# Attention issued from a dated list, with mirrored blocks loaded whole, in a float32 attention and two feed-forward stages on one core

## The chip, the cores and the metric

The kernel runs on one core of a Trainium2 chip. The metric is the device time of one execution in microseconds (us). Five instruction streams run beside each other: TensorE (PE, with its weight loads shown as PEld), VectorE (DVE), ScalarE (ACT), the sync engine (SP, which here only issues DMAs), and GpSimd (POOL, unused but for six instructions). Each stream runs its instructions strictly in the order in which the program lists them; an instruction that has to wait holds up all behind it on its engine.

## The reference

There are two batches of 3008 rows; z has 64 columns, v and u have 256. Scores are taken of z against itself, so the score matrix is symmetric.

```python
scores = (z @ z.T) / S                 # S = 3008
attn   = np.maximum(scores, 0.0) ** 2
x      = u * (attn @ v)                # (2*3008, 256)
h = np.maximum(x @ w_in, 0.0);  x = (h * h) @ w_out            # 2048 hidden columns
h = x @ w2_in;                  y = (h - np.tanh(h)) @ w2_out  # 2048 hidden columns
```

The weights of both feed-forward stages come in float64; the rest is float32.

## The kernel before

Every product of two float32 values is made of three matmuls on operands of TensorE's rounded type fp32r: a value a is split into h (the rounded value) and l = a - h, and h*h, h*l and l*h are summed in PSUM. Splitting is work for ACT (a copy with rounding, or a DVE cast) and DVE (the subtraction).

**Attention.** The 3008 query columns of a batch are cut into six chunks (t = 0 to 5) of 512 columns, the last of 448; with two batches there are twelve chunks. A chunk has twelve *steps*, one for each pair of blocks of 128 keys. A step ends in `values` (24 matmuls into four PSUM banks, 18 for the last pair). What `values` multiplies is made in one of two ways:

- A **scored** step: `scores` (6 matmuls, L508), ACT Relu from PSUM (L520), ACT Square (L544), the rounded copy h on ACT (L548) or DVE (L556), the rest l on DVE (L557). Where the chunk lies left of the diagonal, `put` stores the squared block in DRAM (`ad`).
- A **mirrored** step: since the matrix is symmetric, a chunk t takes its first 2t pairs from what earlier chunks stored. `get` (L463) loads the pair from `ad` with four DMAs, DVE turns it in blocks of 32x32 (`turn`, L472), ACT makes h (L477), DVE makes l (L492).

So chunk t has 12 - 2t scored and 2t mirrored steps, 84 and 60 in all. At a chunk's end ACT and DVE copy the four banks to SBUF (L596, L597), DVE adds the two halves (L600) and multiplies by u (L603), and the product goes to DRAM (`xd`).

**Beside attention** run the splits of v and z, and of the feed-forward weights: one *weight unit* is 128 hidden columns of one stage, loaded as float64 words, decoded and split by six DVE and three ACT instructions (L232 to L245). There are 32 units. The first 6 stay in SBUF, the next `KEEP0 + KEEP1` = 14 are made during attention and kept in DRAM (`wd`), and the last 12 are made while the feed-forward stage runs.

**Order.** The main loop goes through the steps; `scores` runs `APART` = 2 steps ahead of `values`, `get` `XAHEAD` = 3 steps ahead of its use. The side work stands in lanes (z, x, v, weights), from which `fill` takes instructions between those of a step, at a pace worked out from due times.

**Feed-forward.** 192 steps of the first stage (`m1`) and 192 of the second (`m2`), 12 matmuls each (`front` L629, `back` L697); `m1` runs 21 steps ahead, then the two alternate.

Of the kernel before, what the change touches and what calls it, by code (L numbers as in the profile page):

```python
# [17 lines left out]
P = 128  # L18
NMAX = 512
LOOK = 3  # L20
APART = 2
# [4 lines left out]
NW, NZ, NRAW = 32, 7, 3  # L26
# [3 lines left out]
STAY, KEEP0, KEEP1 = 6, 6, 8  # L30
XAHEAD = 3
# [10 lines left out]
def kernel(  # L42
# [58 lines left out]
    for t in range(NC):  # L101
        old, own = list(range(2 * t)), list(range(2 * t, NV))
        own = own[2:] + own[:2] if t else own
        spots = {(2 * k + 1) * NV // (2 * len(old)) for k in range(len(old))}
        if 2 in spots:
            spots = (spots - {2}) | {min(set(range(3, NV)) - spots)}
        plist.append([(old if x in spots else own).pop(0) for x in range(NV)])
# [14 lines left out]
    for i in range(len(m2)):  # L122
# [17 lines left out]
        (b, t, k): dp.tile([qch[k][1], NMAX], F32, name="ad")  # L140
# [6 lines left out]
    def load_v(b, j):  # L147

        if b == 0 and 3 <= j < 6:
            raw = rawp.tile([P, 2, D], F32, tag="raw", name="vraw")  # L150
        else:
            raw = ap_.tile([P, 2, D], F32, tag="a", name="vraw")
        if j < NV - 1:
            order = "(p k) d -> p k d" if j < 2 * (NC - 1) else "(k p) d -> p k d"
            SP.dma_start(
                out=raw, in_=v[b, 2 * j * P : 2 * (j + 1) * P, :].rearrange(order, p=P)
            )
# [25 lines left out]
    def split_z(b, t, raw):  # L183
        z = zp.tile([P, 2, NMAX], F32R, tag="z", name="z")
        zt[b, t] = z
# [8 lines left out]
    def load_w(m, f, keep):  # L194
        win, wout = ((w1_in, w1_out), (w2_in, w2_out))[m]
        cols = slice(f * P, (f + 1) * P)
        if win.dtype == F32:
            raw = rawp.tile([P, 512], F32, tag="raw", name="wraw")
# [6 lines left out]
        raw = rawp.tile([P, 1024], U32, tag="raw", name="wraw")  # L205
# [10 lines left out]
    def split_w(m, f, keep, raw):  # L216
        if keep is None:
# [28 lines left out]
        if keep is not None:  # L246
# [6 lines left out]
    def new_xs(m, c):  # L253
        xs[m, c] = tuple(zp.tile([P, KD, NMAX], F32R, tag="z", name=x) for x in ("xh", "xl"))
        return xs[m, c]

    def load_x(c):
# [3 lines left out]
        return x  # L261

    def split_x(c, x):
        n = chunks[c][2]
        xh, xl = new_xs(0, c)
        yield "A", lambda: A.activation(xh[:, :, :n], x[:, :, :n], AF.Copy)
# [55 lines left out]
    v_units, z_units, x_units, k_units = [], [], [], []  # L322
    by_hand = {("z", 0), ("z", 1), ("z", 2), ("v", 0), ("v", 1)}
    for b in range(B):
        base, end = at["att", b * NC, 0], at["att", (b + 1) * NC - 1, 0]
        for j in range(NV):
            start = 0 if b == 0 else at["att", b * NC - 1, 0] + j + APART
            if b or ("v", j) not in by_hand:
                v_units.append((base + j + 1, start, load_v, split_v, (b, j), 2))
        for t in range(NC):  # L330
            i = b * NC + t
            start = 0 if b == 0 else base - 6 + 2 * t
            if b or ("z", t) not in by_hand:
                z_units.append((base + 2 * t, start, load_z, split_z, (b, t), 2))

# [4 lines left out]
    def weights(ids, first, last):  # L340
        for k in ids:
            k_units.append((last, first, load_w, split_w, (*order[k], keeps.get(k)), 9))
    nv = at["att", NC, 0]
    weights(range(STAY + KEEP0), 10, nv - NV)
    split = STAY + KEEP0 + KEEP1
    weights(range(STAY + KEEP0, split), nv + 6, at["m1", 0, 0] - 2)

    end = at["att", NCH - 1, 0]
    for i, k in enumerate(range(STAY, len(order))):
        m, f = order[k]  # L350
        start = end + max(i + APART + 1, 7) if i < NV else at["m1", 0, 0] + 2
        if k < split:
            fetches.append((start, m, f, keeps[k]))
        else:
            k_units.append((at[("m1", "m2")[m], 0, f], start, load_w, split_w, (m, f, None), 9))
    for c in range(NCH):
        need = at["m1", c, 0]
        free = need - 8 if c == 0 else at["m1", c - 1, 0] + 4
        x_units.append((need, free, load_x, split_x, (c,), 3))
    lane_z, lane_v = Lane(z_units, 2, 1), Lane(v_units, 3, 2)  # L360
    lanes = [lane_z, Lane(x_units, 1, 1), lane_v, Lane(k_units, NRAW, 2)]
# [21 lines left out]
    got = {}  # L383
    single = {}
# [42 lines left out]
    def load_u(i):  # L427

        _, c, x = steps[i]
        b, q, n = chunks[c]  # L430
        if x == 4:
            xt[c] = xp.tile([P, KD, NMAX], F32, tag="x", name="x")
            t0 = b * S + q
            SP.dma_start(
                out=xt[c][:, :, :n],
                in_=uT[:, t0 : t0 + n].rearrange("(k p) t -> p k t", p=P),
            )

    def put(i, a):
# [3 lines left out]
        k = p // 2  # L443
        if k == t:
            return
        r0, tail = p % 2 * 2 * P, p == NV - 1
        rows = ad[b, t, k][r0 : min(r0 + 2 * P, qch[k][1]), :]
        if tail:
            SP.dma_start(out=rows[:P], in_=a[:, 0, :])
            SP.dma_start(out=rows[P:], in_=a[:TAIL, 1, :])  # L450
        else:
            order = "(p k) q -> p k q" if k < NC - 1 else "(k p) q -> p k q"
            SP.dma_start(out=rows.rearrange(order, p=P), in_=a)

    def get(i):

        _, c, _ = steps[i]
        b, t, p = c // NC, c % NC, pair_of(i)
        nb = chunks[c][2] // 32
# [4 lines left out]
        got[i] = m  # L464

    def turn(i):

        _, c, _ = steps[i]
        n = chunks[c][2]
        m = got.pop(i)  # L470
        a = wp.tile([P, 2, NMAX], F32, tag="w", name="at")
        V.transpose(  # L472
            a[:, :, :n].rearrange("p g (k j) -> p k g j", j=32),
            m[:, : n // 32, :].rearrange("p k (i g) -> p k g i", g=2),
        )
        h = wp.tile([P, 2, NMAX], F32R, tag="w", name="ht")
        A.activation(h[:, :, :n], a[:, :, :n], AF.Copy)  # L477
        got[i] = (a, h)

    def low(i):  # L480

        _, c, _ = steps[i]
        n = chunks[c][2]
        a, h = got.pop(i)
        l = wp.tile([P, 2, NMAX], F32R, tag="w", name="l2")
        pair[i] = (h, l)
        credit[0] = min(4, credit[0] + pace(i))
        if late:
            late.popleft()()
        else:  # L490
            credit[0] -= fill(i, min(2, math.ceil(credit[0])), "VS")
        V.tensor_sub(l[:, :, :n], a[:, :, :n], h[:, :, :n])  # L492
        credit[0] -= fill(i, min(2, math.ceil(credit[0])), "A")

    def scores(i):
# [19 lines left out]
        a = wp.tile([P, 2, NMAX], F32, tag="w", name="a2")  # L515
        if i == 0:
            A.activation(a[:, 0, :], both[0], AF.Relu, scale=scale)
            V.tensor_scalar(a[:, 1, :], both[1], scale, 0.0, op0=ALU.mult, op1=ALU.max)
        else:
            A.activation(a[:, :, :n], s[:, :, :n], AF.Relu, scale=scale)  # L520
        return a

    def squares(i, a):

        _, c, x = steps[i]
        n = chunks[c][2]
        full = a
        a = a[:, :, :n]
        h = hp.tile([P, 2, NMAX], F32R, tag="h", name="h2")
        l = wp.tile([P, 2, NMAX], F32R, tag="w", name="l2")  # L530
        pair[i] = (h, l)
        if i == 0:

            A.activation(h[:, 0, :], a[:, 0, :], AF.Square)
            first("z", 1)
            V.tensor_mul(a[:, 1, :], a[:, 1, :], a[:, 1, :])
            first("v", 0)
            A.activation(a[:, 0, :], a[:, 0, :], AF.Square)
            V.tensor_copy(h[:, 1, :], a[:, 1, :])
            first("v", 0)  # L540
            for g in (1, 0):
                V.tensor_sub(l[:, g, :], a[:, g, :], h[:, g, :])
            return
        A.activation(a, a, AF.Square)  # L544
        put(i, full)
        turned = c % NC > 1 or c % NC == 1 and x % 2
        if turned:
            A.activation(h[:, :, :n], a, AF.Copy)  # L548
        credit[0] = min(4, credit[0] + pace(i))

        if late:
            late.popleft()()
        else:
            credit[0] -= fill(i, min(2, math.ceil(credit[0])), "VS")
        if not turned:
            V.tensor_copy(h[:, :, :n], a)  # L556
        V.tensor_sub(l[:, :, :n], a, h[:, :, :n])  # L557
# [275 lines left out]
```

## Time and profile before

| | |
|---|---|
| median of 3 runs | 1577.77 us (1576.92 to 1579.72) |
| profiled execution: its own time | 1580.93 us |
| its span, first to last instruction | 1579.1 us |
| attention: up to the first matmul of `m1` (L629) | 521.7 us |
| feed-forward: from there to the end | 1057.4 us |
| PE busy | 1510.7 us (96%), 8512 matmuls |
| DVE, ACT busy | 1227.6 us (78%), 1057.1 us (67%) |

The profiled execution is one run of its own; its time is 3.2 us above the median. Busy time counts any moment at which an instruction of the engine runs. [...]

### The profile page before, as it was taken

Reading aid. Unit: us, or ns where it says so; the run is one execution under the profiler, and the core shown is the slowest. Engines: PE = TensorE matmul, PEld = TensorE weight load, DVE = VectorE, ACT = ScalarE, POOL = GpSimd, SP = SyncE. Lnnn points to the kernel's source line nnn. Section 1 sums busy time; section 2 is a strip of 40 time slices with the busy share of each in tenths; the row PEclk is TensorE's granted clock in tenths of the full one; section 3 lists DMA queues with packets and bytes.
Section 4 is the critical chain, followed back from the end, with each engine's and each line's share of the span. In section 5 each row is a group of like instructions: output and inputs, shape, how many; then the busy total and the mean of one; then the engine's idle time right before and its main releaser. Section 6 shows DMA issues by size and latency. Waiting matters only on the chain.

```text
span 1579.1 us, 22289 instructions
## 1 busy us (share of the span) xinstructions
PE 1510.7 (96%) x8512; PEld 1250.7 (79%) x8512; DVE 1227.6 (78%) x1897; ACT 1057.1 (67%) x1664; POOL 0.3 (0%) x6
## 2 busy tenths in 40 slices
PE   9989888999888999689999999999999999999999
PEld 7767667777677888578888888888888888888888
DVE  7777778787666689667877788877778787778788
ACT  8777656777654577456766666666666676666688
POOL 0000000000000000000000000000000000000000
PEclk9999999999999999899999999999999999999999
DMA  7767877777797521000000000000000000000000
GB/s 245 222 185 179 195 185 186 233 223 210 185 201 190 185 67 42 12 27 1 26 1 1 27 0 28 0 28 0 26 1 27 1 26 1 1 14 1 14 1 26
DMA packets 166698, 127.27 MB, mean 81 GB/s; under 512 B 126144, under 2 KB 137792, under 8 KB 166592
## 3 DMA queue, kind: packets, MB, share of 16 engines
q1 hardware_dynamic: 166288, 125.48, 28.5%
q8 instruction: 66, 1.08, 0.3%
q10 hardware_dynamic: 304, 0.38, 0.1%
q14 instruction: 40, 0.33, 0.1%
HBM read 76.02 MB, written 49.81 MB: 80 GB/s over the span
## 4 chain that ended last, share of the span: by engine, by line
PE 76%; DVE 6%; ACT 6%; DMA 5%; SPq 4%; issue 2%; DVEq 0%; ACTq 0%
PE s L629 33%; PE o L697 32%; PE o L584 9%; DMA m<-ad 4%; SPq L463 3%; DVE at L472 2%; ACT a L544 2%; PE s L508 2%; ACT h L548 1%; ACT ht L477 1%; DVE l L557 1%; DVE l L492 1%; DMA zraw<-in_z_dram 1%; DVE e L597 0%; DVE mant L242 0%
## 5 line engine op out<-in xcount | busy, mean ns | idle before, releaser
L697 PE MATMUL o<-h,ww 128*128 128x512 f32 (+1 forms) x2304 | 579.2, 387 | 0.0
L697 PEld LDWEIGHTS o<-h,ww 128*128 128x128 f32 x2304 | 435.0, 189 | 83.1 <-DVE h L677 0.5
L629 PE MATMUL s<-xh,ww 128*128 128x512 f32 (+1 forms) x1536 | 408.2, 388 | 17.4 <-ACT ww L244 14.8
L629 PEld LDWEIGHTS s<-xh,ww 128*128 128x128 f32 x1536 | 289.6, 189 | 73.6 <-ACT ww L244 16.0
L584 PE MATMUL o<-l,vw 64*128 64x512 f32 (+1 forms) x1128 | 236.5, 402 | 20.9 <-DVE l L557 12.3
L644 DVE TENSOR_TENSOR h<-a,h 128x512 fp32r<-128x512 f32 (+1 forms) x192 | 130.6, 680 | 141.4 <-ACT h L642 141.1
L584 PE MATMUL o<-h,vw 64*128 64x512 f32 (+1 forms) x1296 | 211.4, 402 | 24.8 <-ACT h L548 19.3
L629 PE MATMUL s<-xl,ww 128*128 128x512 f32 (+1 forms) x768 | 235.0, 387 | 0.0
L637 ACT ACTIVATE a<-s 128x512 f32<-128x512 f32 (+1 forms) x192 | 113.0, 589 | 180.7 <-PE s L629 179.6
L656 ACT ACTIVATE f<-s 128x512 f32<-128x512 f32 (+1 forms) x192 | 114.5, 596 | 129.0 <-PE s L629 129.0
L584 PEld LDWEIGHTS o<-h,vw 64*128 64x128 f32 x1296 | 129.2, 191 | 59.5 <-ACT h L548 27.2
L629 PEld LDWEIGHTS s<-xl,ww 128*128 128x128 f32 x768 | 145.0, 189 | 27.3
L557 DVE TENSOR_TENSOR l<-a,h 128x1024 fp32r<-128x1024 f32 (+1 forms) x83 | 101.2, 1219 | 82.5 <-ACT h L548 81.2
L584 PEld LDWEIGHTS o<-l,vw 64*128 64x128 f32 x1128 | 117.7, 191 | 56.0 <-DVE l L557 25.8
L659 DVE TENSOR_TENSOR a<-s,a 128x512 f32<-128x512 f32 (+1 forms) x192 | 130.4, 679 | 37.8 <-ACT a L657 25.6
L584 PE MATMUL o<-ht,vw 64*128 64x512 f32 (+1 forms) x960 | 150.4, 385 | 0.0
L477 ACT ACTIVATE ht<-at 128x1024 fp32r<-128x1024 f32 (+1 forms) x60 | 61.6, 1027 | 122.8 <-DVE at L472 119.6
L675 DVE COPY_PREDICATED a<-small,f 128x512 f32<-128x512 uint8 (+1 forms) x171 | 126.9, 742 | 5.5
L638 ACT ACTIVATE a<-a 128x512 f32<-128x512 f32 (+1 forms) x192 | 119.7, 624 | 6.1
L678 DVE TENSOR_TENSOR h<-a,h 128x512 fp32r<-128x512 f32 (+1 forms) x172 | 117.9, 686 | 5.9
L672 DVE TENSOR_TENSOR f<-s,f 128x512 f32<-128x512 f32 (+1 forms) x171 | 117.2, 685 | 5.8
L658 ACT ACTIVATE f<-f 128x512 f32<-128x512 f32 (+1 forms) x192 | 121.5, 633 | 0.0
(65 smaller groups left out, 1414.9 us busy)
## 6 DMA issues: line engine op xcount, KB each, us to landing
ad<-a SPq DMA_DIRECT2D x50, 512.0 KB, 3.1
m<-ad SPq DMA_DIRECT2D x160, 128.0 KB, 4.1
m<-ad SPq DMA_DIRECT2D x80, 112.0 KB, 4.2
wraw<-in_moe_w_in_dram SPq DMA_DIRECT2D x32, 256.0 KB, 4.2
wraw<-in_moe_w_out_dram SPq DMA_DIRECT2D x32, 256.0 KB, 4.5
wd<-wk SPq DMA_DIRECT2D x14, 512.0 KB, 4.4
ww<-wd SPq DMA_DIRECT2D x14, 512.0 KB, 6.8
vraw<-in_v_dram SPq DMA_DIRECT2D x22, 256.0 KB, 3.9
```

Source lines behind the costliest of these rows:

```text
L557: V.tensor_sub(l[:, :, :n], a, h[:, :, :n])
L584: T.matmul(o[r * KD + d][:, :n], lhsT=w[halves[r], hl, g * D + d * P : g * D + (d + 1) * P], rhs=mv[halves[r], g, :n], start=x == 0 and (r ...
L629: T.matmul(s_, lhsT=w[:, hl, kd * P : (kd + 1) * P], rhs=mv[:, kd, :n], start=j == 0, stop=j == len(seq) - 1,)
L638: A.activation(a_, a_, AF.Square)
L644: main.append(lambda: V.tensor_sub(l[:, :n], a_, h[:, :n]))
L656: A.activation(f_, s_, AF.Tanh, scale=TB)
L658: A.activation(f_, f_, AF.Square, scale=TC)
L659: main = [lambda: V.tensor_sub(a_, s_, a_)]
L672: main.append(lambda: V.tensor_mul(g_, s_, f_))
L675: late.append(lambda: V.copy_predicated(a_, mask, g_))
L678: late.append(lambda: V.tensor_sub(l[:, :n], a_, h[:, :n]))
L697: T.matmul(o[d][:, :n], lhsT=w[:, side, (KD + d) * P : (KD + d + 1) * P], rhs=mv, start=k == 0 and j == 0, stop=k == NF - 1 and j == len(t ...
```

## The change

In the attention part, the order in which instructions stand on PE, ACT, DVE and SP no longer comes from the main loop and its lanes. Each piece of work is a `Job` with a key (the date at which it is wanted), the jobs that it must follow with a lag, the buffers that it takes and gives back, and a cost on its engine. `drive` walks a model of the four queues in time: whichever engine can start a job first takes the ready one with the smallest key, and only then the instruction is written into the program. The order of PE is a fixed list in which `scores` stands `APART` = 3 steps ahead. A rounded copy of a scored step may go to ACT or DVE, whichever takes it first. The feed-forward part keeps the loop and the lanes.

Further:

- A square of 512 x 512 scores is stored as one DRAM block of 1 MB. `put` writes a pair as four pieces of 1 KB in each partition; `get` loads a whole block, two pairs, with one DMA of 8 KB in each partition. A `turn` reads its pair out of that block with a step of 4 words and writes with a step of 16 words (before: reads with a step of 2, writes runs of 32). In the chunk of 448 columns a `turn` is two instructions of 512. Keys of z are read by the weight loads of `scores` with a step of 4 words (before 2), and rows of v are permuted to match.
- At a chunk's end `values` is cut in two halves by output bank. ACT copies one bank (L603) and DVE adds the other straight from PSUM (L605); the add L600 is gone. For chunks 4 to 11 the product with u moves to the feed-forward stage (`split_x`), which loads u there.
- `KEEP1` goes from 8 to 12: 18 units are kept in DRAM in place of 14, and 8 in place of 12 are made in the feed-forward stage. Pools: 4 z buffers of 8 KB a partition (before 7 of 4 KB), 2 raw buffers (before 3); half of the late weight loads land in the pool `w`.

```diff
-APART = 2
+APART = 3
-NW, NZ, NRAW = 32, 7, 3
+NW, NZ, NRAW = 32, 4, 2
-STAY, KEEP0, KEEP1 = 6, 6, 8
-XAHEAD = 3
+STAY, KEEP0, KEEP1 = 6, 6, 12
+LANES = 8
+EARLY = 4
...
-        (b, t, k): dp.tile([qch[k][1], NMAX], F32, name="ad")
+        (b, t, k): dp.tile([4, P, 4, P], F32, name="ad")
...
+        if c >= EARLY:
+            yield "V", lambda: V.tensor_mul(x[:, :, :n], x[:, :, :n], u[:, :, :n])
         yield "A", lambda: A.activation(xh[:, :, :n], x[:, :, :n], AF.Copy)
...
-        z = z[:, p % 2 * 2 * P : (p % 2 + 1) * 2 * P]
         if p < 2 * (NC - 1):
-            return z.rearrange("r (p k) -> r k p", k=2)[:, g]
-        return z[:, g * P : (g + 1) * P]
+            return z.rearrange("r (p t k) -> r t k p", t=2, k=2)[:, p % 2, g]
+        k = p % 2 * 2 + g
+        return z[:, k * P : (k + 1) * P]
...
-        m = zp.tile([P, 2 * NMAX // 64, 64], F32, tag="z", name="m")
-        rows = ad[b, p // 2, t].rearrange("(k j) (t a x) -> t a j k x", j=32, a=4, t=2)[p % 2]
-        for g in range(4):
-            SP.dma_start(out=m[g * 32 : (g + 1) * 32, :nb, :], in_=rows[g])
...
+        rows = ad[b, t, p // 2].rearrange("a p (t k) x -> t p a (k x)", t=2)[p % 2]
+        SP.dma_start(out=rows, in_=sq[i].rearrange("p a g x -> p a (g x)"))
...
+        m = zp.tile([P, 4 * 4, P], F32, tag="z", name="m")
+        rows = ad[block].rearrange("a (j m) k x -> (a j) (m k x)", m=4)
+        SP.dma_start(out=m.rearrange("p k x -> p (k x)"), in_=rows)
...
+        if c % NC < NC - 1:
+            V.transpose(
+                a.rearrange("p g (j k) -> p k g j", k=16),
+                m.rearrange("p k (i t g) -> t p k g i", t=2, g=2)[p % 2],
+            )
+        else:
+            for g in range(2):
+                V.transpose(
...
+        if e == "A":
+            A.activation(s, o[d][:, :n], AF.Copy)
+        else:
+            V.tensor_add(s, o[KD + d][:, :n], s)
...
+        found = [(max(free[e], ready(j)), j) for j in jobs]
+        start = min(t for t, _ in found)
...
+        soon = [(j.key, t, k) for k, (t, j) in enumerate(found) if t <= start + 0.5]
+        key, t, k = min(soon)
...
+        while any(queue.values()):
+            options = [(*x, e) for e in "PAVS" if (x := best(e)) is not None]
+            t, job, e = min(options, key=lambda x: x[0])
...
+            job.run(e, pools)
+            free[e] = t + cost
+            job.done = t + cost + 0.06
...
+                if block not in blocks:
+                    lim = 1 if t == 1 else 2
...
+                        after.append((blocks[older[-lim]][1], 0.0))
+                    after.append(((max(i - 8, 0)), 0.0))
+                    load = Job(
+                        lambda e, pools: get(block), need - 14.0, after, ["z"], S=3.0
+                    )
```

Where instructions stand now, in three places.

SP, in chunk 4 of the first batch (t = 4), before. L463 is `get`, L434 the load of u, L207 and L211 the loads of a weight unit, L247 its store:

```order
L604 DMA xd<-x 128x1024
L463 DMA m<-ad 32x16x64 x4
L434 DMA x<-in_u_dram 128x2x512
L247 DMA wd<-wk 128x1024
L207 DMA wraw<-in_moe_w_in_dram 128x2x256
L211 DMA wraw<-in_moe_w_out_dram 128x512
L463 DMA m<-ad 32x16x64 x8
L247 DMA wd<-wk 128x1024
L463 DMA m<-ad 32x16x64 x4
L463 DMA m<-ad 32x14x64 x8
```

The same place of the changed kernel; L446 is `get`, L215 and L219 load and L974 stores a weight unit:

```order
L616 DMA xd<-x 128x1024
L215 DMA wraw<-in_moe_w_in_dram 128x2x256
L219 DMA wraw<-in_moe_w_out_dram 128x512
L974 DMA wd<-wk 128x1024
L446 DMA m<-ad 128x2048 x2
L974 DMA wd<-wk 128x1024
```

Before, each pair of blocks takes four loads; now one load brings two pairs, and weight stores stand between the loads.

ACT in the same chunk, before, from one scored step's Relu (L520) to its rounded copy (L548); L477 is the rounded copy of a mirrored step, L234 and L235 belong to a weight unit:

```order
L477 ACTIVATE ht<-at 128x1024
L234 ACTIVATE mant<-mant 128x512
L235 ACTIVATE exp<-exp,ebias 128x512
L520 ACTIVATE a_2497<-s 128x1024
L477 ACTIVATE ht<-at 128x1024
L544 ACTIVATE a_2497<-a_2497 128x1024
L548 ACTIVATE h_2527<-a_2497 128x1024
```

ACT around the corresponding scored step of the changed kernel; L507 is the Relu, L518 the Square, L487 the rounded copy of either kind:

```order
L507 ACTIVATE a_2500<-s 128x2x4x128
L518 ACTIVATE a_2500<-a_2500 128x1024
L487 ACTIVATE h_2509<-at 128x1024
L487 ACTIVATE h_2535<-a_2500 128x1024
L487 ACTIVATE h_2541<-at 128x1024
L242 ACTIVATE mant<-mant 128x512
L243 ACTIVATE exp<-exp,ebias 128x512
```

Before, a mirrored step's copy stands between the Relu and the Square of a scored step; now the Square follows the Relu, and a mirrored step's copy stands behind the Square.

DVE in the first chunk of the feed-forward stage, before, with the eleventh weight unit made there (L232 to L245) between the instructions of an `m1` step (L644) and `m2` steps (L659 to L678):

```order
L644 TENSOR_TENSOR h<-a,h 128x512
L677 CAST h<-a 128x512
L678 TENSOR_TENSOR h<-a,h 128x512
L232 TENSOR_SCALAR mant<-wraw 128x512
L233 TENSOR_SCALAR exp<-wraw 128x512
L236 SCALAR_TENSOR_TENSOR mant<-wraw,mant 128x512
L239 SCALAR_TENSOR_TENSOR exp<-wraw,exp 128x512
L242 TENSOR_TENSOR mant<-mant,exp 128x512
L245 TENSOR_TENSOR ww<-mant,ww 128x512
```

The changed kernel where its eighth and last unit there ends (L253):

```order
L658 TENSOR_TENSOR h<-a,h 128x512
L691 CAST h<-a 128x512
L692 TENSOR_TENSOR h<-a,h 128x512
L253 TENSOR_TENSOR ww<-mant,ww 128x512
L673 TENSOR_TENSOR a<-s,a 128x512
L685 TENSOR_SCALAR small<-f 128x512
```

Counted in `m1` steps on DVE, the last units before end behind the 33rd, 34th, 35th and 36th step, each whole unit in one place; the eight units now end behind the 11th, 12th, 17th, 20th, 25th, 28th, 31st and 34th.

## Rows read from the trace of the kernel before

**Rows 1.** Stretches (from:to): length; busy PE, PEld, DVE, ACT, POOL; clock, DMA share, GB/s.

```profile
0.00:521.70 521.70, 474.30 (x3905) 381.06 (x3905) 384.86 (x449) 344.33 (x398) 0.33 (x6) 0.97 0.76 203
...
640.00:720.00 80.00, 62.63 (x240) 49.72 (x239) 53.97 (x92) 41.25 (x72) 0.00 (x0) 0.87 0.04 14
720.00:1560.00 840.00, 840.00 (x3778) 708.75 (x3777) 672.10 (x1145) 573.46 (x1022) 0.00 (x0) 1.00 0.03 11
```

**Rows 2.** PE in order of time, early in chunk 0 (start, us, instruction).

```profile
8.54 2.11 PE L584 MATMUL o<-h,vw 64*128 64x512 f32 x16 [0.23 <-ACT vw L169]
...
15.03 0.86 PE L508 MATMUL s<-z 64*128 64x512 f32 x6
15.72 1.07 PE L584 MATMUL o<-h,vw 64*128 64x512 f32 x8
...
18.45 0.86 PE L508 MATMUL s<-z 64*128 64x512 f32 x6
```

**Rows 3.** Columns of rows 1, for chunks 2 to 5, 6, 7, 8, and 8 to 11.

```profile
90.73:266.66 175.93, 153.54 (x1244) 120.99 (x1246) 132.90 (x155) 110.07 (x131) 0.00 (x0) 0.96 0.79 191
...
266.66:307.45 40.79, 40.61 (x356) 33.28 (x354) 33.38 (x42) 32.62 (x39) 0.00 (x0) 1.00 0.75 249
307.45:348.95 41.50, 40.21 (x348) 32.09 (x344) 32.13 (x39) 32.11 (x36) 0.00 (x0) 1.00 0.60 194
348.95:389.51 40.56, 38.81 (x328) 31.31 (x326) 29.41 (x34) 33.63 (x38) 0.00 (x0) 1.00 0.74 212
348.95:521.10 172.15, 152.51 (x1236) 124.52 (x1234) 115.63 (x122) 97.79 (x110) 0.00 (x0) 0.95 0.77 197
```

**Rows 4.** What PE waited for in attention (us in total, times, longest).

```profile
PE o L584 <- ACT h L548: 19.3, 16, 2.9
PE o L584 <- DVE l L557: 12.3, 24, 0.5
```

**Rows 5.** All engines in order of time, a stall in chunk 4.

```profile
205.13 1.25 DVE L472 STREAM_TRANSPOSE at<-m 128x1024 f32<-128x1024 f32 x1 [2.31 <-DMA m<-ad]
...
206.46 1.06 ACT L477 ACTIVATE ht<-at 128x1024 fp32r<-128x1024 f32 x1 [3.10 <-issue]
...
207.42 1.04 ACT L544 ACTIVATE a<-a 128x1024 f32<-128x1024 f32 x1
208.49 1.06 ACT L548 ACTIVATE h<-a 128x1024 fp32r<-128x1024 f32 x1
...
209.60 0.73 PE L584 MATMUL o<-h,vw 64*128 64x512 f32 x4 [2.92 <-ACT h L548]
```

**Rows 6.** Instructions of line 463: least, median, most ns on SP; first and last start.

```profile
L463 SPq DMA_DIRECT2D m<-ad x240: 303/541/1997, 42.9 to 507.3; - x120
```

**Rows 7.** What PE waited for from 640 to 720 us.

```profile
PE s L629 <- ACT ww L244: 14.8, 3, 5.7
PE s L629 <- DVE ww L245: 2.6, 1, 2.6
```

**Rows 8.** DMA issues by kind: count, size of one, median us to landing.

```profile
ad<-a SPq DMA_DIRECT2D x50, 512.0 KB, 3.1
...
ww<-wd SPq DMA_DIRECT2D x14, 512.0 KB, 6.8
```

**Rows 9.** Groups of DVE instructions (busy us, mean ns, idle before).

```profile
L671 DVE TENSOR_SCALAR small<-f 128x512 uint8<-128x512 f32 x155 | 64.8, 418 | 0.0
...
L472 DVE STREAM_TRANSPOSE at<-m 128x1024 f32<-128x1024 f32 x40 | 49.6, 1240 | 8.8 <-DMA m<-ad 8.8
...
L236 DVE SCALAR_TENSOR_TENSOR mant<-wraw,mant 128x512 f32<-128x512 uint32 x32 | 21.6, 682 | 0.0
...
L232 DVE TENSOR_SCALAR mant<-wraw 128x512 uint32<-128x512 uint32 x32 | 13.3, 417 | 2.9 <-DMA wraw<-in_moe_w_out_dram 2.9
...
L600 DVE TENSOR_TENSOR e<-e 128x1024 f32<-128x1024 f32 x10 | 12.3, 1226 | 1.0
```

**Rows 10.** The weight loads of `scores` (ns, least, median, most).

```profile
L508 PEld LDWEIGHTS s<-z x504: 184/190/314, 4.9 to 498.1; 64*128 64x128 f32 x168
```

More of the change, by code (lines that the diff above doesn't have):

```diff
@@ L320, in pop @@
             return op
[L322 to L334, printed above, removed]
+    x_units, k_units = [], []
     order = [(m, f) for m in range(2) for f in range(NF)]
@@ L350 @@
         m, f = order[k]
[L351 removed]
+        start = at["m1", 0, 0] + 2
         if k < split:
@@ L476, in turn @@
[L476 to L484, printed above, removed]
-        l = wp.tile([P, 2, NMAX], F32R, tag="w", name="l2")
[L486 to L493, printed above, removed]
+        p = pair_of(i)
@@ L514, in scores, with values @@
                 )
[L515 to L557, printed above, removed]
-        credit[0] -= fill(i, min(2, math.ceil(credit[0])), "A")
-    def values(i):
+        got[i] = both if i == 0 else s
+    def values(i, part):
         _, c, x = steps[i]
@@ L582, in values @@
         for y, (g, j, r, d) in enumerate(seq):
+            if part is not None and part != (g == 0 and d == 1 if p == NV - 1 else d == 1):
+                continue
             hl, mv = terms[j]
@@ L727, in back, with __init__ @@
                 )
+    class Job:
+        def __init__(self, run, key, after=(), take=(), give=(), **cost):
+            self.run, self.key, self.cost = run, key, cost
+            self.after, self.take, self.give = list(after), list(take), list(give)
+            self.done = None
+            for e in cost:
+                queue[e].append(self)
+            for hold in self.give:
+                hold[1] += 1
+    queue = {"P": [], "A": [], "V": [], "S": []}
+    free = {"P": 0.0, "A": 1.5, "V": 2.5, "S": 1.0}
@@ new lines, with hold, ready @@
+    room = {
+        "w": [0.0] * (NW - 6),
+        "h": [0.0, 3.0],
+        "z": [0.0, 0.0],
+        "x": [0.0] * 2,
+        "raw": [0.0] * NRAW,
+        "t": [0.0] * 6,
+        "a": [0.0] * 3,
+        "s": [0.0, 1.0],
+        "o": [0.0] * 4,
+    }
+    spots = {"w": wp, "h": hp}
+    wire = [0.0]
+    sent = []
+    def hold(pool):
+        return [pool, 0, 0.0]
+    def ready(job):
+        t = 0.0
+        for before, lag in job.after:
+            if not isinstance(before, Job):
+                before = done.get(before)
+            if before is None or before.done is None:
+                return 1e9
+            t = max(t, before.done + lag)
+        for pool in set(job.take):
+            times, k = room[pool], job.take.count(pool)
+            if pool == "h":
+                times = sorted(times + room["w"][:1])
+            if len(times) < k:
+                return 1e9
+            t = max(t, times[k - 1])
+        if "S" in job.cost and len(sent) >= LANES:
+            t = max(t, sent[-LANES])
+        return t
@@ new lines, in best @@
+    def best(e):
+        jobs = queue[e]
+        if not jobs:
+            return None
+        if e == "P":
+            return (max(free[e], ready(jobs[0])), jobs[0])
+        found = [(max(free[e], ready(j)), j) for j in jobs]
+        start = min(t for t, _ in found)
+        if start >= 1e9:
+            return None
+        late = free["P"] - reached[0]
+        soon = [(j.key, t, k) for k, (t, j) in enumerate(found) if t <= start + 0.5]
+        key, t, k = min(soon)
+        if t > start and key + late > t + 0.6:
+            key, t, k = min(x for x in soon if x[1] <= start)
+        return (t, found[k][1])
@@ L755 @@
             first(*x)
-        mirrors = [i for i in range(len(steps)) if mirrored(i)]
-        ahead = asked = 0
-        for n in range(-1, len(steps)):
-            if n < 0:
-                until = 1
-            elif n < at["m1", 0, 0]:
-                until = min(n + APART, at["m1", 0, 0] - 1)
-            else:
-                until = n + (LOOK if n < end else FAR)
-            todo = []
+        scores(0)
+        opening(got.pop(0))
+        scores(1)
+        relu(1)
+        square(1)
+        cast(1, "V", hp)
+        low(1)
+        for x in (("v", 1), ("z", 2)) * 2:
+            first(*x)
+        asked.append(Job(lambda e, pools: None, 0.0, S=0.0))
+        queue["S"].pop()
+        asked[0].done = 0.0
+        plan((v_loaded, z_loaded))
+        ahead = at["m1", 0, 0]
+        for n in range(ahead, len(steps)):
+            until = n + (LOOK if n < end else FAR)
             while ahead <= min(until, len(steps) - 1):
```

510 lines of the change are left out of this document (403 added, 107 removed).

## Prediction

> **What bounds the kernel now.** I read the busy times by stretch first. TensorE is the bound, but with two leaks. Attention takes 521.7 us with PE busy for 474.3 of them at a mean clock of 0.97; from 640 to 720 us PE is busy for only 62.6 of 80 at 0.87; from 720 us on it is busy without a gap at 1.00 [rows 1]. Nothing in this change touches the matmuls of that last stretch, so the question is how much of the two leaks goes.
>
> The size of the first leak comes from PE's own order of time. Early in chunk 0, where nothing is late, a scored step takes 18.45 - 15.03 = 3.42 us: 0.69 for `scores` and 2.73 for `values` [rows 2]. A full chunk then needs 11 x 2.73 + 2.05 (18 of 24 matmuls in the last pair) = 32.1 us for `values`, and 0.69 for each scored step; a chunk of 448 columns 0.875 of that. Over a batch that is 5 x 32.1 + 28.1 + 0.69 x 41.75 = 217.4, over both 434.8. PE starts with `values` at 8.54 us [rows 2], when three `scores` (2.1) are done. So with no wait attention would end at 8.5 + 434.8 - 2.1 = 441 us; 81 us are lost. That is more than the idle time, since matmuls behind a stall also run slower.
>
> Where it is lost, the chunks show [rows 3]. Chunk 6 (all scored) takes 40.79 against 32.1 + 8.3 = 40.4: nothing lost. Chunk 7 takes 41.50 against 39.0 and chunk 8 takes 40.56 against 37.6: 2.5 and 3.0. Chunks 2 to 5 and 8 to 11, with most mirrored steps, take 175.9 + 172.2 = 348 against 2 x (37.6 + 36.2 + 34.9 + 29.3) = 276: 72 lost. In those DVE is busy 132.9 + 115.6 = 248 us and ACT 208, less than PE's 276. No engine is too slow; they wait for each other.
>
> How, one stall shows. PE's waits in attention lead with the rounded copy h of scored steps on ACT (19.3 us) and l on DVE (12.3) [rows 4]. In the stall of chunk 4 a turn on DVE waits 2.31 us for its block from DRAM. The mirrored copy L477 stands behind it on ACT and cannot start before 206.46, though the Square of a scored step, which needs neither, stands next in ACT's queue. That Square runs at 207.42, its copy at 208.49, and PE has waited 2.92 us at 209.60 [rows 5]. The block is late because of SP: `get` is 240 issues of 0.54 us in the median and up to 2.0 [rows 6], 130 us of one in-order queue, of which four stand before each pair.
>
> The second leak has its own cause: PE waits 14.8 + 2.6 us for weight units [rows 7]. The stretch holds 240 matmuls; at the later rate of 3778 in 840 us it would hold 360 [rows 1]. The 120 missing are 26.7 us, 17.4 of waiting and the rest lower clock.
>
> **The change part by part.**
>
> *Loads of mirrored blocks.* 240 issues become 30, so about 113 us of issuing leave SP, in the chunks where the wait begins. Packets grow from 256 bytes to 8 KB. One block of 1 MB does not appear in the trace. From below, 512 KB land in 3.1 us (the stores), from above 512 KB in 6.8 (weights loaded in a burst), doubled 13.6 [rows 8]. I take 6, since the loads stand eight steps ahead and not in a burst.
>
> *Order.* The stall above comes from a mirrored copy ahead of a Square. ACT's new order has the Square directly behind the Relu, the casts go to whichever engine is free, and `scores` is three steps ahead. How much of the 81 us this returns no row can say. All of it gives 441. If every one of the twelve chunks still loses what chunks 7 and 8 lose today, when few blocks are waited for, (2.5 + 3.0) / 2 = 2.75 each, it gives 441 + 33 = 474. I take the middle, 457.5: a gain of 521.7 - 457.5 = **64 us**.
>
> *Does the work still fit?* Four more weight units in attention are six DVE instructions each, two of 0.417 and four near 0.682 [rows 9], 3.6 us, so 14 us. Against that go ten full and two short adds L600 at 1.226 [rows 9], 14.5, and eight products of about the same length, 9.6. A 448-column pair has two turns of 512 in place of one of 896; by columns of the 1240 ns full turn [rows 9] that is 1.24 to 1.3 against 1.09 on 20 pairs, 4 us. DVE goes from 385 [rows 1] to about 379 of 457 us, 83%. ACT gains twelve instructions of 512 columns; at no more than the 1.06 of 1024 columns [rows 5] that is below 13 us, to 357 at most. The copies at a chunk's end keep their number. The eight products return in the feed-forward stage, where DVE is busy 672 of 840 us [rows 1]; 10 us hide there, and without that room would cost PE at most 10.
>
> *Turn and keys with larger steps.* A turn takes 1240 ns now with reads at a step of 2 words [rows 9]. Rows do not show a step of 4 or 16. Such a step of 2 is free where it can be seen: L232 takes 417 ns with it, L671 takes 418 on runs [rows 9]. I take 1240, and double it for the far end. The weight loads of `scores` take 190 ns [rows 10] beside 0.69 / 3 = 0.23 us a pair of matmuls; doubled to 380 they would add 0.15 three times a step, on the 60 scored steps with such keys 27 us. I take nothing, with the same reason. [...]
>
> *Weight units in feed-forward.* Eight in place of twelve. Today the first eight are in time and PE loses nothing up to 640 us; the ninth to twelfth are late. The new eight end on DVE behind the 11th to 34th `m1` step, and the last is wanted by the 36th. I take the whole 26 us back. Against it, nine stored units of 512 KB now stand on SP ahead of the first weight load, and the first decode stands behind the fifth `m1` step on DVE, ahead of casts that PE wants. At 512 KB in 3.1 us each [rows 8] that load may be some us late: 3 us, between 0 and 8. Sum: **23 us**.
>
> *Sum.* The profiled execution took 1580.9 us, 1.8 outside its span. 1580.9 - 64 - 23 = 1494, and the median lies 3.2 below that execution: **1490 us**.
>
> **The rivals.**
>
> 1. *Two block buffers are too few.* A load may start only when both turns of the block two before are done. A block feeds 2 x 2.73 = 5.5 us of PE. A cycle of two blocks, 10.9 us, must hold landing and two turns some 4 us apart: 6 + 4 fits, 13.6 + 4 = 17.6 does not. Each block would then last 8.8 us; in chunks 5 and 11 (five blocks, 29.3 us of PE work, two scored steps) that is 44 us, 15 lost in each, elsewhere scored steps cover it. 1490 + 30 = 1520. For it: nothing lands faster per byte than 512 KB in 3.1. Against: loads are one DMA of long packets on an emptier queue.
>
> 2. *Turns take twice as long.* Chunks 2 to 5 and 8 to 11 hold 36 full turns and 40 of 512 columns (half of 1.24 and a little, 0.65): 36 x 1.24 + 40 x 0.65 = 71 us more on DVE, 248 + 71 = 319 against PE's 276. DVE becomes the bound there: attention 441 + 43 + 16 (the same loss) = 500, total 1577.8 - 22 - 23 = 1533. [...]
>
> 3. *Slower: turns take three times as long*, as if the step of 4 on the read and of 16 on the write each cost a whole pass. DVE has 390 us in those chunks, attention 441 + 114 + 16 = 571, total 1577.8 + 49 - 23 = 1604. It decides from the point where 441 + 16 + the excess reaches 521.7 + 23, an excess of 88: 364 - 248 = 116 us over turns worth 57 full ones, 2.0 each, a turn of 3.3 us. Against: the free step of 2.
>
> 4. *The order does not do what it says*: loads come early but the static queues stall elsewhere as much as now, and only the weights gain: 1578 - 23 = 1555.
>
> **How the numbers follow.** The forecast, attention between 441 and 474 and 18 to 26 us from the weights, spans 1474 to 1505: 0.66. Rival 1, 1505 to 1528: 0.16. Rival 2: 0.07. Rival 4: 0.04. Slower, rival 3: 0.04. Below 1474 0.02; no difference 0.01. The range 1474 to 1528 holds 0.82. A measurement of this kernel can tell about 0.2%, 3 us: faster 0.95, the same 0.01, slower 0.04.
>
> **What would show it.** The first matmul of `m1` between 441 and 474 us; waits of PE for h and l of attention below 20 us in all; turns of 1.24 us on full chunks and about 0.65 on halves; weight loads of `scores` at 190 ns; 30 block loads landing in 5 to 7 us; no wait for a decoded weight around 570 to 620 us. I am wrong if a turn is over 2 us, if DVE waits for blocks in chunks 3 to 5 and 9 to 11, or if PE's idle time in attention stays near the 47 us of now [rows 1] with other releasers.

## The result, and the profile after

The changed kernel takes 1500.06 us against 1578.74 us: a ratio of 0.950, interval 0.948 to 0.952. (One of its four runs, 2471 us at a granted TensorE clock of 0.56 of full speed, is left out of the ratio but counted in this median; the other three have a median of 1499.45.) The forecast was 1490, range 1474 to 1528: 78.7 us came where 87.8 were forecast. The two profiled executions lie 80.3 us apart, and there the two terms of the sum came out as 54.7 us (attention, forecast 64) and 25.6 us (feed-forward, forecast 23). The first of them hides two errors that partly cancelled.

The same stretches as [rows 1], of the changed kernel: attention, the start of the feed-forward stage, the stretch in which the old one stalled, and the rest.

```profile
0.00:467.00 467.00, 453.61 (x3904) 387.56 (x3904) 426.50 (x477) 342.79 (x408) 0.33 (x6) 0.99 0.69 231
467.00:560.00 93.00, 92.77 (x410) 76.45 (x409) 71.72 (x134) 63.90 (x109) 0.00 (x0) 1.00 0.34 119
560.00:640.00 80.00, 80.00 (x355) 66.26 (x354) 69.63 (x120) 55.57 (x98) 0.00 (x0) 1.00 0.06 20
640.00:1480.00 840.00, 840.00 (x3777) 708.93 (x3776) 680.52 (x1153) 573.82 (x1022) 0.00 (x0) 1.00 0.04 15
```

Attention ends at 467.0 us in place of 521.7, and behind it PE runs almost without a gap up to 1480 us. What is new is DVE: it is busy for 426.5 of 467 us, where the forecast counted 379.

What PE waited for in attention, to be read beside [rows 4]:

```profile
PE o L588 <- DVE l L496: 6.8, 8, 2.2
PE o L588 <- DVE e L605: 2.8, 5, 1.0
PE o L588 <- ACT e L603: 2.3, 3, 1.4
```

The waits for h of scored steps on ACT, 19.3 us before, are gone; all that is left comes from DVE or a chunk's end. PE's idle time in attention falls from 47.4 to 13.4 us. The loads answer to [rows 6, 8]. Before, DVE waited for blocks 14 times (us in total, times, longest):

```profile
DVE at L472 <- DMA m<-ad: 24.4, 14, 4.7
```

Now it never waits for one. Their issue on SP (least, median, most ns):

```profile
L446 SPq DMA_DIRECT2D m<-ad x30: 319/424/980, 31.8 to 441.8; - x30
```

and by kind (count, size of one, median us to landing):

```profile
ad<-a SPq DMA_DIRECT2D x60, 512.0 KB, 4.2
m<-ad SPq DMA_DIRECT2D x30, 1024.0 KB, 6.5
```

A block of 1 MB lands in 6.5 us; I had taken 6. The turns answer to [rows 9] (busy us, mean ns, idle before):

```profile
L456 DVE STREAM_TRANSPOSE at<-m 128x1024 f32<-128x1024 f32 x40 | 82.1, 2052 | 0.0
...
L462 DVE STREAM_TRANSPOSE at<-m 128x512 f32<-128x512 f32 x40 | 42.1, 1120 | 0.0
```

and the weight loads of `scores` to [rows 10] (least, median, most ns):

```profile
L551 PEld LDWEIGHTS s<-z x504: 184/305/334, 4.9 to 448.3; 64*128 64x128 f32 x168
```

A full turn takes 2052 ns in place of 1240, one of 512 columns 1120, and a weight load of keys 305 ns in the median in place of 190. Both had been forecast to cost nothing. Where the longer turns bite, the chunks show (chunks 4, 5, 6 and 11, columns as in [rows 3]):

```profile
165.97:203.33 37.36, 36.29 (x295) 29.97 (x297) 37.27 (x39) 22.17 (x28) 0.00 (x0) 0.95 0.62 217
203.33:242.90 39.57, 35.36 (x314) 32.03 (x312) 37.48 (x42) 24.13 (x31) 0.00 (x0) 0.96 0.49 163
242.90:283.10 40.20, 40.20 (x352) 34.20 (x352) 35.92 (x47) 35.98 (x46) 0.00 (x0) 1.00 0.88 294
...
434.08:467.00 32.92, 30.36 (x288) 26.61 (x287) 30.56 (x33) 14.92 (x18) 0.00 (x0) 1.00 0.69 256
```

In chunk 4 DVE is busy for 37.27 of 37.36 us, and the chunk is as long as DVE's work. Chunk 5, with ten mirrored steps, loses 10 us against the 29.3 that PE needs; chunk 6, all scored, loses nothing.

### The profile page after: what moved, and what is told of

It is laid out like the page before. It is cut to its first block, busy times and chain, and to the rows that moved or that the text cites. A ratio compares the mean times of both kernels' runs of the same rounds, so it can differ in the third digit from the quotient of the medians.

```text
span 1498.8 us, 22087 instructions
## 1 busy us (share of the span) xinstructions
PE 1481.7 (99%) x8512; PEld 1252.5 (84%) x8512; DVE 1262.8 (84%) x1907; ACT 1048.9 (70%) x1662; POOL 0.3 (0%) x6
## 4 chain that ended last, share of the span: by engine, by line
PE 84%; DVE 10%; DMA 2%; ACT 2%; issue 2%; SPq 0%; DVEq 0%; ACTq 0%
PE o L711 34%; PE s L643 34%; PE o L588 14%; DVE at L456 3%; PE s L551 3%; DVE l L496 2%; DVE at L462 2%; ACT h L487 1%; DMA wraw<-in_moe_w_out_dram 1%; DMA zraw<-in_z_dram 1%; DMA wd<-wk 0%; DVE e L605 0%; DMA ww<-wd 0%; DVE wk L253 0%; DMA vraw<-in_v_dram 0%
## 5 line engine op out<-in xcount | busy, mean ns | idle before, releaser
L643 PE MATMUL s<-xs,ww 128*128 128x512 f32 (+1 forms) x2304 | 575.2, 385 | 0.0
L643 PEld LDWEIGHTS s<-xs,ww 128*128 128x128 f32 x2304 | 432.5, 188 | 81.1 <-issue 0.3
L588 PE MATMUL o<-h,vw 64*128 64x512 f32 (+1 forms) x2256 | 380.4, 387 | 5.2 <-DVE e L605 2.8
L588 PEld LDWEIGHTS o<-h,vw 64*128 64x128 f32 x2256 | 280.9, 186 | 44.1 <-DVE e L605 6.3
L588 PE MATMUL o<-l,vw 64*128 64x512 f32 (+1 forms) x1128 | 296.5, 387 | 6.9 <-DVE l L496 6.8
L651 ACT ACTIVATE a<-s 128x512 f32<-128x512 f32 (+1 forms) x192 | 113.0, 589 | 173.2 <-PE s L643 171.4
L588 PEld LDWEIGHTS o<-l,vw 64*128 64x128 f32 x1128 | 172.1, 186 | 29.4 <-DVE l L496 10.9
L487 ACT ACTIVATE h<-at 128x1024 fp32r<-128x1024 f32 (+1 forms) x60 | 61.5, 1024 | 93.2 <-DVE at L456 36.4
L671 ACT ACTIVATE a<-s 128x512 f32<-128x512 f32 (+1 forms) x192 | 113.9, 593 | 0.0
L656 ACT ACTIVATE h<-a 128x512 fp32r<-128x512 f32 (+1 forms) x171 | 106.4, 622 | 5.5
L518 ACT ACTIVATE a<-a 128x1024 f32<-128x1024 f32 (+1 forms) x83 | 87.1, 1052 | 1.2
```

The source lines that it names most:

```text
L588: T.matmul(o[r * KD + d][:, :n], lhsT=w[halves[r], hl, g * D + d * P : g * D + (d + 1) * P], rhs=mv[halves[r], g, :n], start=x == 0 and (r ...
L643: T.matmul(s_, lhsT=w[:, hl, kd * P : (kd + 1) * P], rhs=mv[:, kd, :n], start=j == 0, stop=j == len(seq) - 1,)
```

## The experiments

Times are medians; "against the changed kernel" means against 1500.06 us. The kernel before, run again beside the experiments, had medians of 1577.2, 1577.3 and 1577.6 us where it had 1578.74 beside the result, so a difference of one or two us is not clear of that drift, and one of 3 us is at the edge. The first matmul of `m1` marks the end of attention, as before.

**Turns on runs.** Both sides of each turn read and write runs of 32 words; the blocks land in other columns than the reference wants.

```diff
-                a.rearrange("p g (j k) -> p k g j", k=16),
-                m.rearrange("p k (i t g) -> t p k g i", t=2, g=2)[p % 2],
+                a.rearrange("p g (k j) -> p k g j", k=16),
+                m.rearrange("p k (t g i) -> t p k g i", t=2, g=2)[p % 2],
...
```

The two views of the short turns are changed in the same way.

> The changed kernel with both sides of every turn on runs of 32 words; the blocks then stand in the wrong columns, so only the time is read. My theory: the changed kernel's turn is slow (2052 ns on 1024 columns, 1120 on 512) because of its steps of 4 and 16 words, and this is what the forecast missed; here a turn takes about 1240 and 650 ns, 40 x 0.81 + 40 x 0.47 = 51 us leave DVE, and the first matmul of m1 comes near 457.5 us, as forecast, so the time falls by about 9 us against the changed kernel. Rival: DVE's time for turns lies beside PE's work, and attention's last 26 us above 441 have another cause; then turns are as short but the time stays within 3 us.

1480.99 us (ratio to before 0.939, 0.937 to 0.941): 19.1 below the changed kernel, twice what I expected. The turns are short, as the groups of this run show:

```profile
L456 DVE STREAM_TRANSPOSE at<-m 128x1024 f32<-128x1024 f32 x40 | 49.5, 1239 | 0.0
...
L462 DVE STREAM_TRANSPOSE at<-m 128x512 f32<-128x512 f32 x40 | 25.6, 685 | 0.0
```

Its attention ends at 447.4 (columns as in [rows 1]):

```profile
0.00:447.40 447.40, 445.45 (x3905) 382.87 (x3905) 381.31 (x477) 342.69 (x408) 0.33 (x6) 1.00 0.72 241
```

With them DVE is busy 381 us, which the forecast had at 379, and attention stands only 6 us above the 441 that PE's rows give. So the slow turns cost 19.6 us of attention, and the order loses less than I thought. The weight loads of `scores` are as in the changed kernel, 272 ns in the mean in both.

**Which side of the turn.** Only the write on runs (read still at a step of 4), and only the read on runs (write still at 16, or 4 in the short turns); the blocks land in other columns here too. The diffs are the two lines above, one each, with the same side of the short turns.

> Reads at a step of 4 words as in the changed kernel, writes on runs of 32 (output in the wrong columns). If the read's step is the cost, a turn takes about 2050 ns as now; if the write's step is, about 1240; if both share it, between.

> Reads on runs of 32, writes at a step of 16 words (4 in the turns of 512) as in the changed kernel (output in the wrong columns). If the write's step is the cost, about 2050 ns; if the read's is, about 1240. In the changed kernel a turn of 512 columns takes 1120 ns with a write step of 4, so if the write alone cost, 512 columns would show it at 4 words already.

Full turns (least, median and most ns): the changed kernel with both steps, then only the read at 4, then only the write at 16:

```profile
L456 DVE STREAM_TRANSPOSE at<-m x40: 2009/2058/2103, 46.7 to 422.5; 128x1024 f32<-128x1024 f32 x40
```

```profile
L456 DVE STREAM_TRANSPOSE at<-m x40: 1983/2024/2051, 46.7 to 420.4; 128x1024 f32<-128x1024 f32 x40
```

```profile
L456 DVE STREAM_TRANSPOSE at<-m x40: 1932/1976/2024, 46.4 to 418.8; 128x1024 f32<-128x1024 f32 x40
```

Either side alone costs nearly all of it (2024 and 1976 against 2058 with both and 1239 with neither, medians). They do not add, so mending one side is worth little: a single run of each took 1498.1 and 1495.2 us, 2 and 5 below the changed kernel, where mending both gave 19. The short turns agree: 1074 ns with only the read at 4 words and 1086 with only the write at 4, against 1120 with both and 672 with neither (medians).

**True costs in the list.** The list's cost of a turn set to the measured one.

```diff
-                    V=1.25 if f == 1 else 1.4,
+                    V=2.05 if f == 1 else 2.24,
```

> The changed kernel, with the list's cost of a turn set to what the trace shows (2.05 and 2 x 1.12 in place of 1.25 and 1.4); only the order changes. My theory: the list stacks DVE work behind turns that it thinks short, so dates slip; with true costs PE waits less and the time falls by 2 to 6 us. Rival: DVE is simply full in the mirrored chunks, the order cannot help, and the time stays within 2 us.

1501.63 us, 1.6 above the changed kernel, which is no clear difference: my theory fell and the time is the rival's. The rival's reason is not shown with it. The list took 6 us of work from DVE (busy 420.5 us in attention), and still PE's waits for l, 6.8 us before, grew:

```profile
PE o L588 <- DVE l L496: 13.2, 18, 2.3
```

**The weight units undone.**

```diff
-STAY, KEEP0, KEEP1 = 6, 6, 12
+STAY, KEEP0, KEEP1 = 6, 6, 8
```

> The changed kernel with KEEP1 back at 8, so that twelve weight units are made in the feed-forward stage. My theory: the feed-forward stage loses its 26 us again (waits of PE for decoded weights of some 15 us and a lower clock behind them), while attention, with 14 us less work on DVE, gets some 5 to 10 us shorter: net 15 to 20 us slower than the changed kernel. Rival: in the new order the late units fit anyway, no wait comes back, and the time falls by the 5 to 10 us.

1526.13 us, 26.1 above the changed kernel. What PE waits for shows the old stall, to the tenth, in the new order:

```profile
PE s L643 <- ACT ww L252: 14.8, 3, 5.7
...
PE s L643 <- DVE ww L253: 2.6, 1, 2.6
```

The first half of my theory held. The second did not: attention ends at 467.6, as with the four units. In this run DVE is idle for 5.6 to 11.7 us in each of chunks 6 to 9, and in the changed kernel each of these four makes one unit more than here and no other chunk does. So the units lie in room that DVE has.

**The weight units alone,** in the kernel before: `KEEP1 = 12` and nothing else.

> The kernel before with KEEP1 = 12 alone. My theory: the feed-forward stage is 26 us shorter than before, and the old attention, where DVE waits more than it works, takes the four units almost for nothing (0 to 8 us): 18 to 26 us faster than before. Rival: the gain of the weights needs the new order, the units lengthen the old attention by their 14 us or more and the sum is within 10 us of before.

1566.73 us, 10.6 below before (ratio 0.993, 0.992 to 0.995); neither number was met. The profiled execution, 1564.7, shows the two parts (columns as in [rows 1]):

```profile
0.00:530.00 530.00, 472.16 (x3905) 374.47 (x3905) 396.30 (x473) 350.69 (x410) 0.33 (x6) 0.98 0.77 208
530.00:1562.90 1032.90, 1028.01 (x4610) 864.68 (x4608) 829.82 (x1425) 705.61 (x1254) 0.00 (x0) 1.00 0.06 21
```

The feed-forward stage is 24.5 us shorter, the old attention 8.3 longer. The two profiled executions are 16.2 us apart and the medians only 10.6, so by the medians the four units cost the old attention more, some 14 us if the feed-forward stage gains the same. They cost the old order 8 us or more, and the new one nothing that can be seen. So the parts of the change do not simply add: the weights alone give 10.6 us, all the rest without them (`KEEP1 = 8`) 52.6, and both together 78.7.

**Old loads in the new order.** Each block in eight DMAs of 256-byte packets.

```diff
-        SP.dma_start(out=m.rearrange("p k x -> p (k x)"), in_=rows)
+        rows = rows.rearrange("p (k x) -> p k x", x=P)
+        for g in range(4):
+            for h in range(2):
+                part, cols = slice(g * 32, (g + 1) * 32), slice(h * 64, (h + 1) * 64)
+                SP.dma_start(out=m[part, :, cols], in_=rows[part, :, cols])
```

> The changed kernel with each block loaded by eight DMAs of 256-byte packets, as many issues and as small packets as before, in the new order. My theory before: 113 us of issuing on SP is what made blocks late, so block loads land late again and DVE waits for them; 10 to 30 us slower than the changed kernel. Rival: the order, which asks for a block eight steps ahead, covers slow loads too; within 4 us of the changed kernel.

1502.77 us, 2.7 above the changed kernel, at the edge of what can be told: the rival. SP issues 240 loads again, and DVE waits for a block once, for 0.6 us:

```profile
L450 SPq DMA_DIRECT2D m<-ad x240: 538/626/2771, 31.9 to 453.5; - x120
```

```profile
DVE l L500 <- DMA m<-ad: 0.6, 1, 0.6
```

So in the new order, which asks for a block up to eight steps ahead, the issuing that left SP is not what pays. Two things stay untried: the new loads in the old order, and the old order with its loads asked for earlier than three steps ahead.

**One rule of the old order.** A Square waits in the list for the rounded copy of the mirrored step behind it, with the new loads and then with the old ones.

```diff
+                behind = [(up, 0.0)]
+                if x < NV - 1 and mirrored(i + 1):
+                    behind.append((("copy", i + 1), 0.0))
                 ready_a = Job(
-                    lambda e, pools: square(i), need - 3.8 * f, [(up, 0.0)], (), [], A=1.06 * f
+                    lambda e, pools: square(i), need - 3.8 * f, behind, (), [], A=1.06 * f
...
+            if mirrored(i):
+                done["copy", i] = ready_h
```

> The changed kernel with one rule of the old order put back: the Square of a scored step may be listed on ACT only behind the rounded copy of the mirrored step that follows it. My theory: this coupling of ACT to DVE's turn, and of the turn to the load, is where the old attention lost its 81 us, so PE waits for h of scored steps return and the time rises by 10 to 40 us. Rival: with the loads early and everything else dated, one rule costs little; within 4 us of the changed kernel.

> Both parts of the old chain in the new order: the rule of the run copy_first and the eight 256-byte-packet loads of the run load8. My theory: late loads alone were covered (load8 cost 2.7 us over the changed kernel), since ACT no longer passed them on; with the rule they reach PE, and this run loses clearly more than the sum of the two apart. Rival: they add up, so loads stay without effect in this schedule.

1511.11 us, 11.0 above the changed kernel, the low end of what I expected, and waits of PE for h on ACT are back:

```profile
PE o L588 <- DVE l L496: 10.3, 12, 1.6
PE o L588 <- ACT h L487: 4.5, 3, 2.5
```

With the old loads as well, 1516.98 us, 16.9 above: 3.2 more than the two apart (11.0 + 2.7). "Clearly more than the sum" was not met: the runs of either kernel with the rule spread over 4 us. Nor could it show lateness carried to PE, for almost no load was late; DVE waited for a block once:

```profile
DVE at L466 <- DMA m<-ad: 1.3, 1, 1.3
```

**No dates.** The list's choice without its keys.

```diff
-        soon = [(j.key, t, k) for k, (t, j) in enumerate(found) if t <= start + 0.5]
+        soon = [(0.0, t, k) for k, (t, j) in enumerate(found) if t <= start + 0.5]
         key, t, k = min(soon)
-        if t > start and key + late > t + 0.6:
+        if False and t > start and key + late > t + 0.6:
```

The second change switches off the other place where the choice looks at a key.

> The changed kernel with the dates left out of the list's choice: each engine takes whichever job can start first in the model. My theory: side work (weight units, splits of v and z) then pushes ahead of work that PE wants next, and attention gets 10 us or more longer. Rival: readiness alone orders well enough, and the buffers and gates hold the rest; within 4 us of the changed kernel.

1521.76 us, 21.7 above the changed kernel. The largest of PE's waits:

```profile
PE o L588 <- DVE e L605: 11.0, 8, 2.7
PE s L551 <- DVE z L199: 7.8, 1, 7.8
PE o L588 <- DVE l L496: 7.3, 5, 4.4
```

Work that PE wants at a certain moment, the sums at a chunk's end and the split of z for the second batch, comes late: as expected.

**Scores two steps ahead** (`APART = 2`).

> The changed kernel with scores two steps ahead of values in place of three. My theory: a scored step's chain on ACT and DVE (1.0 + 1.05 + 1.06 + 1.2 us and the copies between) needs the third step where turns fill DVE; 3 to 15 us slower. Rival: the dates already hold the chain in time and the second pair of PSUM banks is the limit; within 3 us.

1504.30 us, 4.2 above: as expected.

**A version with short turns.** The new order and sums, with the tokens of a pair laid out as before, so that keys and turns are read at a step of 2 and turns write runs; the whole reference is computed. ACT's Relu writes groups of 64 columns apart, a block is stored in pieces of 1 KB (512 bytes for the last two pairs) and loaded by four DMAs of 512-byte packets; the list's cost of a short turn is set to 1.12.

```diff
-            return z.rearrange("r (p t k) -> r t k p", t=2, k=2)[:, p % 2, g]
+            return z.rearrange("r (p k) -> r k p", k=2)[:, g]
...
-            a.rearrange("p a g x -> p g a x"),
-            s.rearrange("p g (a x) -> p g a x", a=4),
+            a.rearrange("p a g t x -> p (g t) a x"),
+            s.rearrange("p g (t a x) -> p (g t) a x", t=2, a=4),
...
-        rows = ad[block].rearrange("a (j m) k x -> (a j) (m k x)", m=4)
-        SP.dma_start(out=m.rearrange("p k x -> p (k x)"), in_=rows)
+        rows = ad[block].rearrange("a (k j) x -> a j k x", j=32)
+        for g in range(4):
+            SP.dma_start(out=m[g * 32 : (g + 1) * 32], in_=rows[g])
...
+            a[:, :, :n].rearrange("p g (k j) -> p k g j", j=32),
+            m[:, : n // 32].rearrange("p k (t i g) -> t p k g i", t=2, g=2)[p % 2],
```

> The new order and PSUM sums, with rows laid out so that turns read at a step of 2 words and write runs, and keys are read at a step of 2, as before; a block is stored in pieces of 1 KB and loaded with four DMAs of 512-byte packets. It computes the whole reference. My theory: turns take 1240 and about 1100 ns (one of 896 again), attention ends near 447 us as with turns on runs, and the time is near 1481 us, 19 below the changed kernel. Rival: the smaller packets and 120 loads cost in landing what the turns give, and the time stays above 1490.

1479.40 us (ratio to before 0.938, 0.937 to 0.940), 20.7 below the changed kernel and the fastest here. Its turns, by groups:

```profile
L460 DVE STREAM_TRANSPOSE at<-m 128x1024 f32<-128x1024 f32 x40 | 49.5, 1237 | 1.4 <-DMA m<-ad 1.4
L460 DVE STREAM_TRANSPOSE at<-m 128x896 f32<-128x896 f32 x20 | 21.7, 1099 | 0.0
```

its weight loads of `scores`:

```profile
L549 PEld LDWEIGHTS s<-z x504: 183/190/195, 4.8 to 429.0; 64*128 64x128 f32 x168
```

and its attention (columns as in [rows 1]):

```profile
0.00:447.00 447.00, 444.08 (x3909) 386.61 (x3910) 376.11 (x456) 345.30 (x411) 0.33 (x6) 1.00 0.92 242
```

The first matmul of `m1` stands at 445.9 us, PE has 3 us of idle time before it, and DVE waits 1.4 us in all for its smaller packets. Both slow accesses are gone here, the turns and the weight loads. With turns on runs, where only the first was gone, attention ended 1.5 us later (the block loads differ as well).

## Why the prediction was right, and where not

**The two leaks** were read rightly. In the best version attention ends 5 us above the 441 worked out from one undisturbed step, so that bound was good to about 1%.

**The number is partly luck.** 1500 lies in the forecast's own part of the range, and attention's 467.0 us between 441 and 474, but not for the reason given. Attention had a gain of 64 us on record; the order and all that came with it gave 74.3, and the turns, forecast to cost nothing, took 19.6 back. Of my signs of being wrong one came true: a turn is over 2 us.

**Order, 64 us, was mis-sized.** I took the middle between 441 and 474. With turns at the length that I had assumed, attention ends at 447.4: the order, the loads and the sums return 74.3 us of the 81. The upper end, "every chunk loses what chunks 7 and 8 lose today", was no fair neighbour, I think, since those chunks had the old order's coupling too; no run tests that.

**Turn and keys at nothing: this is the step that failed.** "I take 1240" and, for the keys, "I take nothing, with the same reason" leaned on a step of 2 being free and stretched it to 4 and 16. The turn went to 2052 ns, 1.65 times, and a short one to 1120 against 685 on runs, 1.6 times; the weight loads went to 305 ns, 1.6 times. No row of before shows a larger step, so both prices of nothing were my estimates. The runs show what it costs: a turn that reads at a step of 2 words takes 1237 ns and one on runs 1239, but 2024 with a read step of 4. Of the two slower accesses one is paid: DVE's turns cost attention 19.6 us. The other is hidden, as PE's order of time early in chunk 0 of the changed kernel shows:

```profile
22.78 0.87 PE L551 MATMUL s<-z 64*128 64x512 f32 x6
23.48 1.09 PE L588 MATMUL o<-h,vw 64*128 64x512 f32 x8
...
26.23 0.87 PE L551 MATMUL s<-z 64*128 64x512 f32 x6
```

The six matmuls of `scores` still take 0.70 us, and the step 3.45 against the 3.42 of [rows 2]. By the prediction's own working, a load of 305 ns beside 0.23 us a pair would have added 0.07 three times, 0.2 us a step; 0.03 came. So that price was wrong as well, in the other direction.

The rival "turns take twice as long", whose factor of two was my estimate, was right that longer turns make DVE the bound, at a smaller size (1.65 times). In the stretches that it names, chunks 2 to 5 and 8 to 11, DVE is now busier than the 276 us that PE needs, 282 of 299 us (319 in its sum):

```profile
89.17:242.90 153.73, 146.68 (x1257) 126.98 (x1257) 147.21 (x155) 102.30 (x123) 0.00 (x0) 0.98 0.60 207
322.17:467.00 144.83, 139.83 (x1237) 117.36 (x1235) 134.86 (x138) 94.09 (x109) 0.00 (x0) 1.00 0.65 228
```

Its 1533 us came from a price of 43 us for the turns, where 19.6 were paid, and from 16 us of lost order, where 6 were left.

**Loads.** Landing was sized well (6.5 against 6), and the two buffers were enough: that rival is out. (The reason "nothing lands faster per byte than 512 KB in 3.1" had missed a row: the stores of the output, 512 KB each, landed in 2.8 before.) But the causal step "the block is late because of SP" does not carry the gain: with old issues and packets in the new order 2.7 us are lost, not 10 to 30, and blocks are not late. That a late block hurts through the queues of DVE and ACT, which pass its lateness on to work that does not need it, is what the one stall of [rows 5] shows (a block waited for 2.31 us on DVE, PE idle for 2.92 us behind it); how much of the 81 us went that way, and how much is won merely by asking for blocks earlier, is not shown.

**Work that fits.** DVE at 379 us was about right for turns of 1240 ns (381 with turns on runs). The ends summed from PSUM were not tested apart; their effect is only argued, from the 14.5 us of adds that left DVE.

**Weights, 23 us,** came out at 25.6, the whole 26 without the 3 us taken off for a late load. The first decode on DVE did wait for its load, as feared:

```profile
486.42 0.43 DVE L240 TENSOR_SCALAR mant<-wraw 128x512 uint32<-128x512 uint32 x1 [6.32 <-DMA wraw<-in_moe_w_out_dram]
```

But PE was busy for 92.77 of the 93 us around it: the steps that it runs ahead covered the wait. The run with `KEEP1 = 8` brings back the same waits, 14.8 and 2.6 us, as [rows 7].

**What stays open.** No single rule holds the old 81 us. In the new schedule the dates are worth 21.7 us, one old rule 11.0, old loads 2.7, the third step of lead 4.2; 39.6 us if they simply added, about half, and each was tried alone against a schedule in which the rest was new. How they add in the old one was not tried.

## What to carry to other kernels

When a new layout buys longer DMA packets, look at what it does to the word step of every compute access, on both sides: in the new order long packets were worth some 3 us at most, and the price of the layout on VectorE was 20. A transfer that is asked for early enough may be slow: with eight small loads a block VectorE waited 0.6 us. Before making a transfer faster, look also at what is queued behind the wait without needing it; one such rule cost 11 us here. And a moved piece of work costs nothing only if the order puts it where its engine has room. Four weight units were free in the new order, in chunks 6 to 9, and cost 8 us or more in the old one, though VectorE was busy there for only 385 of 522 us; look at the chunks, and not only at the kernel's mean.

## What the runs showed that I had not expected

In these turns the cost of a larger step is paid once: a turn with only its read at a step of 4 words takes 2024 ns, with only its write at 16 words 1976, with both 2058, with neither 1239. And a weight load that is 1.6 times as long (305 ns against 190) left the pace of the matmuls beside it nearly as it was, 3.45 us a step against 3.42.
